# Moving one group's transfers ahead of the weights, and reordering the first two groups of a fused attention and state-space kernel

## The chip, the cores and the metric

The kernel runs on one core of a Trainium2 chip. The time is the device time of one execution in microseconds (us). The engines of the core are PE (TensorE, matrix multiply, with its weight loads shown apart as PEld), DVE (VectorE), ACT (ScalarE), POOL (GpSimd) and SP (SyncE, which here only issues transfers). Each engine works through its own instructions in order. Transfers (DMAs) are issued by SP, ACT or GpSimd and carried out by 16 DMA engines that all of them share.

## What is computed

A gated linear attention over 4 batches, 8 heads, 768 positions and a head size of 48, and then a gated state-space layer on its output:

```python
for t in range(S):                        # attention, per batch and head
    state = alpha[t][:, None] * state + outer(k[t], v[t])
    y[t] = q[t] @ state
x = y.transpose(0, 2, 1, 3).reshape(B, S, H * D)      # (4, 768, 384)
proj = x @ w_in                           # 384 x 1024
val, gate = proj[..., :512], proj[..., 512:]
a = exp(A_log)[0]                         # one decay for all channels
h[t] = a * h[t - 1] + val[t]
out = (silu(gate) * h) @ w_out            # 512 x 384
```

The weights `w_in`, `w_out` and `A_log` arrive as 8-byte words and are turned into float32 on the core.

## The kernel before

**Groups.** The 4 x 768 positions are cut into 12 groups of 256, numbered 0 to 11 (m for the attention of a group, n for its state-space part), each of two chunks (c = 0, 1) of 128 positions. Three groups make one batch.

**Attention of a group.** Alpha, k and q are brought into a layout with head channels on the partitions. For groups 0 to 2 this is done by PE transposes (`natural_alpha`, L572, and `natural_qk`, L589, results called `tn`); from group 3 on DVE transposes (`products`, L616, line L620). `products` then makes running products of alpha (`prod`, the scan of L629) and their inverses (`inv`, the scan of L641), and Z holds k times `inv` and q times `prod` (L603 for groups up to 2, L652 later). Per chunk there follow:

- `keys` (L659): PE turns the k half of Z (`tp`), ACT copies it to `ktm`;
- `scores` (L668): PE multiplies the k half with the q half of Z (`sc`, two PSUM banks);
- `masks` (L678): the causal mask, `A` from `sc`. For group 1 and chunk 1 of group 0 DVE multiplies both banks by the mask (L683). Otherwise ACT copies one bank (L685), GpSimd multiplies that one (L686), and DVE does the other (L687);
- `values` (L689), `state` (L713) and `carried` (L701): PE products that give y and the running state `st`.

**From y to x.** `join` (L724) copies y of a group out of PSUM (`y_sb`, ACT) and writes it in the order of the channels of x as `xT`. Heads 0 and 4 are copied by ACT (L737); the other six need eight moves, since two of them cross a boundary of 128 partitions. These eight are DMAs (L743). Group 0 and group 2 issue them from GpSimd, all others from SP.

**State-space part.** `block(n, cc)` for cc = 0 to 3: `project` (L751) multiplies xT by w_in (`pv`, `pg`), `hidden` (L765) is DVE's scan over time (`hh`, L767), and `gate` (L772) makes f = silu(pg) x hh: ACT and then GpSimd (L778, L779), but for group 0 ACT in place and then DVE (L915, L775). `output` (L786) multiplies f by w_out, copies and stores.

**Weights.** `load_w_in(i)` (L440) issues two DMAs of 384 KB, i = 0 to 3; `load_w_out` (L446) two of 768 KB in all. A weight unit (four of w_in, two of w_out) is rebuilt by `low_word` (ACT, L512), `high_word` (DVE, L526 and L528: two operations, or four through a PSUM bank when `banks` is given) and `word_sum` (GpSimd, L535, one instruction for each half).

**Order.** The order on every engine is written out by hand (a manual schedule): the engines work in the order of the program's text. From the start it is: loads of alpha, k, q, v of groups 0 and 1 and all of w_in on SP (L814 to L824; one chunk of alpha and A_log on ACT); alpha, k, q of group 0; then w_out and alpha of group 2 on SP; attention of group 0 and its `join`; transposes of k and q of group 1, two filler matmuls (`warm`), Z of group 1, words of unit 0, scores, masks and keys of group 1, words of units 1 and 2, `join` of group 1, then SP's loads of k, q and v of group 2; four blocks of group 0 with words of units 3 to 5 between them; alpha of group 2; loads of group 3; `output(0)`. After that a loop runs over n = 1 to 11, in which the attention of group n + 1, the products of group n + 2 and the blocks of group n are interleaved. SP's loads and moves are in one queue, in the order of the text. PSUM tiles with the tag `mm` (pv, pg, o, tp) share three buffers.

Of the kernel before, what the change touches and what calls it, by code (L numbers as in the profile page):

```python
# [13 lines left out]
AF = mybir.ActivationFunctionType  # L14
# [332 lines left out]
def fast(  # L347
# [18 lines left out]
    nc = tc.nc  # L366
    B, H, S, D = q.shape
    DM = H * D
    DI = moe_A_log.shape[0]
    C = 128  # L370
    G = 2
# [68 lines left out]
    def load_w_in(i, engine):  # L440
        for vg in range(2):
            engine.dma_start(out=bits_in[i][:, :, vg].rearrange("p kk n two -> p kk (n two)"),
                             in_=moe_w_in.bitcast(U32)[:, ds(2 * (vg * DI + i * C), 2 * C)]
                             .rearrange("(kk p) n -> p kk n", p=C))

    def load_w_out(i, engine):  # L446
        engine.dma_start(out=bits_out[:, ds(2 * i, 2)].rearrange("p cc n two -> p cc (n two)"),
                         in_=moe_w_out.bitcast(U32)[ds(2 * C * i, 2 * C)].rearrange("(cc p) n -> p cc n", p=C))
# [59 lines left out]
    def low_word(i):  # L508
        lo, _, w = unit(i)
        _, x, y, z = w.shape  # L510
        wrs[i] = p4.tile([C, x, y, z], I32, tag="wr", name="wr")
        nc.scalar.activation(wrs[i], lo, AF.Copy, scale=2.0 ** -29)  # L512

    def high_word(i, banks=None):

        _, hi, w = unit(i)
        t = w.bitcast(U32)
        if banks is None:
            parts = [(hi, t, t)]
        elif i < NI:  # L520
            parts = [(hi[:, :, vg], banks[vg][:, 0:NK], t[:, :, vg]) for vg in range(2)]
        else:
            parts = [(hi[:, r, 0], banks[r].rearrange("p h n -> p (h n)")[:, 0:DM], t[:, r, 0])
                     for r in range(2)]
        for h, x, y in parts:
            nc.vector.tensor_scalar(out=x, in0=h, scalar1=3, scalar2=0x3FFFFFFF,  # L526
                                    op0=ALU.logical_shift_left, op1=ALU.bitwise_and)
            nc.vector.scalar_tensor_tensor(out=y, in0=h, scalar=0xC0000000, in1=x,  # L528
                                           op0=ALU.bitwise_and, op1=ALU.bitwise_or)

    def word_sum(i):
        w, r = unit(i)[2].bitcast(I32), wrs.pop(i)
        for half in range(2):
            x, y = (t[:, :, half] if i < NI else t[:, half] for t in (w, r))
            nc.gpsimd.tensor_tensor(out=x, in0=x, in1=y, op=ALU.add)  # L535
# [132 lines left out]
    def scores(m, c):  # L668
        Z = Zs[m]
        cols = ds(c * C, C)  # L670
        sc = [ps_sc.tile([C, 4, C], FP32, tag=f"sc{i}", name=f"sc{i}") for i in range(2)]
        for p in range(4):
            for i in range(2):
                rows = ds(64 * i, D)
                nc.tensor.matmul(sc[i][:, p, :], Z[rows, p, 1, cols], Z[rows, p, 0, cols], start=True, stop=True)  # L675
        As[m, c] = p2.tile([C, 2, 4, C], FP32, tag="A", name="A"), sc

    def masks(m, c):  # L678
        A, sc = As[m, c]
        mb = mask[:, None, :].to_broadcast([C, 4, C])  # L680
        if m == 1 or (m, c) == (0, 1):
            for i in range(2):
                nc.vector.tensor_mul(A[:, i], sc[i], mb)  # L683
            return
        nc.scalar.activation(A[:, 1], sc[1], AF.Copy)  # L685
        nc.gpsimd.tensor_mul(A[:, 1], A[:, 1], mb)  # L686
        nc.vector.tensor_mul(A[:, 0], sc[0], mb)  # L687
# [33 lines left out]
        S_sbs[ch] = p2.tile([C, 4, D], FP32, tag="S_sb", name="S_sb")  # L721
        nc.scalar.activation(S_sbs[ch], st, AF.Copy)

    def join(m, engine):  # L724

        y = ys.pop(m)
        y_sb = p2.tile([C, 4, GC], FP32, tag="y_sb", name="y_sb")
        nc.scalar.activation(y_sb[:, 1::2], y[1], AF.Copy)
        nc.scalar.activation(y_sb[:, 2], y[0][:, 1], AF.Copy)
        xT = xTs[m] = p2.tile([C, NK, GC], FP32, tag="xT", name="xT")  # L730

        def transfers():
            for h in range(H):
                s, a = divmod(h, 4)
                if not a:
                    kk, row = divmod(h * D, C)
                    nc.scalar.activation(xT[ds(row, D), kk], y[0][ds(64 * s, D), 0], AF.Copy)  # L737
                    continue
                d = 0
                while d < D:  # L740
                    kk, row = divmod(h * D + d, C)
                    size = min(D - d, C - row)
                    engine.dma_start(out=xT[ds(row, size), kk], in_=y_sb[ds(64 * s + d, size), a])  # L743
                    d += size
        return transfers


    prev_h = [None] * NI
# [22 lines left out]

    def gate(n, cc, pg):  # L772
        hh = hhs.pop((n, cc))
        if n == 0:
            nc.vector.tensor_mul(fs[n][:, cc, :], hh, pg)  # L775
            return
        sg = p2.tile([C, GC], FP32, tag="sg", name="sg")
        nc.scalar.activation(sg, pg, AF.Silu)  # L778
        nc.gpsimd.tensor_mul(fs[n][:, cc, :], sg, hh)  # L779
# [29 lines left out]
    def pair(name, m, one, other):  # L809
        load_natural(name, m, 0, one)  # L810
        load_natural(name, m, 1, other)
# [8 lines left out]
    pair("k", 1, SP, SP)  # L820
    pair("q", 1, SP, SP)
    load_v(1, SP)
    for i in range(NI):
        load_w_in(i, SP)  # L824

    constants()
    def warm(count):

        t = ps_mm.tile([C, 4, C], FP32, tag="mm", name="warm")
        for _ in range(count):  # L830
            nc.tensor.matmul(t, ident, ident[:, None, :].to_broadcast([C, 4, C]), start=True, stop=True)
# [9 lines left out]
    nc.scalar.activation(a_dec, al, AF.Exp)  # L841
    check_alpha(0)
    k_times, q_times = natural_qk(0, "k"), natural_qk(0, "q")
    for i in range(2):
        load_w_out(i, SP)
    pair("a", 2, SP, SP)

    warm(2)
    evict = natural_alpha(1)
    warm(2)  # L850
# [19 lines left out]
    values(0, 1)  # L870
    state(0, 1)
    carried(0, 1)
    join(0, nc.gpsimd)()
    k_times, q_times = natural_qk(1, "k"), natural_qk(1, "q", ps_mm)
    warm(2)
    for _ in steps:
        pass
    for times in (k_times, q_times):
        for c in range(G):
            times(c)  # L880
    low_word(0)
    high_word(0)
    word_sum(0)


    for c in range(G):
        scores(1, c)
    for c in range(G):
        masks(1, c)
    for c in range(G):  # L890
        keys(1, c)
    low_word(1)
    state(1, 0)
    values(1, 0)
    banks = [ps_sc.tile([C, 4, C], U32, tag=f"sc{i}", name=f"bank{i}") for i in range(2)]
# [1 line left out]
    def words(i):  # L897
        high_word(i, banks)
        word_sum(i)

    words(1)
    values(1, 1)
    state(1, 1)
# [1 line left out]
    words(2)  # L905
    carried(1, 0)
    carried(1, 1)
    join(1, SP)()
    for name in "kq":
        pair(name, 2, SP, SP)  # L910
    load_v(2, SP)
    for cc in range(NI):
        pv, pg = project(0, cc)
        hidden(0, cc, pv)
        nc.scalar.activation(pg, pg, AF.Silu)  # L915
        if cc < NI - 1:
            low_word(cc + 3)
            words(cc + 3)
        gate(0, cc, pg)
# [9 lines left out]
    for n in range(1, N):  # L929
        m = n + 1  # L930
        att = m < N
        steps = products(n + 2) if n + 2 < N else iter(())

        def go(count):
            for _ in range(count):
                next(steps, None)

        def attend():
            if att:
                state(m, 0)  # L940
                values(m, 0)
                values(m, 1)
                state(m, 1)
                carried(m, 0)
                carried(m, 1)
                join(m, nc.gpsimd if m == 2 else SP)()

        if n == 1:
            block(n, 0)
            k_times, q_times = natural_qk(m, "k"), natural_qk(m, "q")  # L950
            for c in range(G):
                k_times(c)
                q_times(c)
            block(n, 1)

        if n + 3 < N:
            loads(n + 3)
        if n + 2 < N:
            load_v(n + 2, SP)
        if att:  # L960
            for c in range(G):
                keys(m, c)
            for c in range(G):
                scores(m, c)
        go(1)
        if att:
            for c in range(G):
                masks(m, c)
        if n > 1:
            block(n, 0)  # L970
            if n == N - 1:
                next(end, None)
            go(1)
            block(n, 1)
            go(1)
            attend()
            go(2)
            block(n, 2)
        else:
            block(n, 2)  # L980
            go(1)
            attend()
            go(1)
        go(1)
        block(n, 3)
        go(10)
        if 3 <= n:
            for _ in itertools.islice(checks, 2):
                pass
        if n == N - 2:  # L990
            end = check_end()
            next(end)
        if n == N - 1:
            value = nc.values_load(flag[0:1, 0:1], min_val=0, max_val=1)
        output(n)
# [39 lines left out]
```

## Time and profile before

| | us (or as noted) |
|---|---|
| median of 3 runs | 297.95 (297.06 to 298.05) |
| profiled execution, device time | 297.63 |
| its span in the profile | 295.9 |
| PE busy | 286.1 (97%) |
| DVE busy | 227.8 (77%) |
| POOL busy | 108.1 (37%) |
| ACT busy | 98.7 (33%) |
| moved by the queue q1 (SP's), of all DMA bytes | 40.81 MB of 42.08 MB |

A row of the timeline reads: start, length, engine, line of the program, operation, what is written and from what, shape, how many instructions are merged, and in brackets how long the engine was idle before and who ended the wait. An engine name with a q stands for its instruction sequencer, as with SPq, which issues DMAs: there the length is the time that issuing took, not the transfer. "To landing" is the time from issue until all parts of a transfer have arrived.

### The profile page before, as it was taken

How to read it: one execution, taken by the hardware profiler on the slowest of the kernel's cores; microseconds unless marked ns; L12 is line 12 of the kernel's file. 1: busy time of each engine (PE TensorE's matmuls, PEld its weight loads, DVE VectorE, ACT ScalarE, POOL GpSimd, SP SyncE). 2: the span in 40 equal slices, each digit the busy share in tenths (PEclk: the TensorE clock that was granted, in tenths of full speed). 3: DMA queues.
4: the chain of work that ended last, by engine and by line, in shares of the span. 5: the costliest groups of instructions: out<-in, count | busy, mean ns of one | idle time of the engine just before them, and what ended most of it. 6: DMA issues, size and time to landing. Idle time of an engine off the chain costs nothing. (4 is left out here: it accounts for less than half of the span.)

```text
span 295.9 us, 6116 instructions
## 1 busy us (share of the span) xinstructions
PE 286.1 (97%) x2347; PEld 226.7 (77%) x2347; DVE 227.8 (77%) x266; ACT 98.7 (33%) x219; POOL 108.1 (37%) x112
## 2 busy tenths in 40 slices
PE   8899999999999999999999999999999999999991
PEld 4577976986886886886886886886886887886870
DVE  4999897799998599699699699699699695312211
ACT  3354644232531531531531531531531531431110
POOL 7028570166423423453423423452423423401110
PEclk9999999999999999999999999999999999999998
DMA  9999959999991891891891693791694401101101
GB/s 129 163 170 304 350 89 160 231 279 228 242 201 39 218 201 38 206 211 39 213 207 36 172 221 64 201 210 44 166 223 67 109 10 35 53 13 29 53 4 62
DMA packets 71150, 42.08 MB, mean 142 GB/s; under 512 B 47492, under 2 KB 70408, under 8 KB 71112
## 3 DMA queue, kind: packets, MB, share of 16 engines
q1 hardware_dynamic: 69552, 40.81, 67.6%
q0 software_dynamic: 512, 0.59, 0.9%
q8 instruction: 20, 0.33, 0.5%
q10 hardware_dynamic: 1048, 0.20, 0.5%
q14 instruction: 18, 0.15, 0.2%
HBM read 33.33 MB, written 4.72 MB: 129 GB/s over the span
## 5 line engine op out<-in xcount | busy, mean ns | idle before, releaser
L779 POOL TENSOR_TENSOR f<-sg,hh 128x256 f32<-128x256 f32 x44 | 56.1, 1275 | 100.0 <-ACT sg L778 50.7
L759 PE MATMUL pv<-xT,w_in 128*128 128x256 f32 x288 | 72.4, 387 | 0.0
L759 PE MATMUL pg<-xT,w_in 128*128 128x256 f32 x288 | 70.3, 380 | 0.0
L792 PE MATMUL o<-w_out,f 128*128 128x384 f32 x192 | 64.0, 486 | 0.0
L759 PEld LDWEIGHTS pg<-xT,w_in 128*128 128x128 f32 x288 | 54.5, 190 | 8.1 <-DVE hh L767 0.8
L759 PEld LDWEIGHTS pv<-xT,w_in 128*128 128x128 f32 x288 | 52.7, 190 | 10.2 <-issue 2.0
L792 PEld LDWEIGHTS o<-w_out,f 128*128 128x128 f32 x192 | 36.4, 190 | 23.0 <-DVE hh L767 0.2
L686 POOL TENSOR_TENSOR A<-A,mask 128x512 f32<-128x512 f32 x21 | 26.8, 1295 | 66.0 <-ACT A L685 66.0
L778 ACT ACTIVATE sg<-pg 128x256 f32<-128x256 f32 x44 | 16.9, 383 | 89.2 <-PE pg L759 89.2
L767 DVE TENSOR_TENSOR_SCAN hh<-a_dec,hh,pv 128x256 f32<-128x256 f32 x32 | 23.3, 727 | 24.3 <-PE pv L759 24.2
L629 DVE TENSOR_TENSOR_SCAN prod<-aT,first 128x1024 f32<-128x1024 f32 x12 | 33.0, 2753 | 0.1
L641 DVE TENSOR_TENSOR_SCAN inv<-aT,last 128x1025 f32<-128x1025 f32 x12 | 30.6, 2547 | 0.4
L687 DVE TENSOR_TENSOR A<-sc,mask 128x512 f32<-128x512 f32 x21 | 14.3, 689 | 18.5 <-PE sc L675 18.4
L797 ACT ACTIVATE o_sb<-o 128x384 f32<-128x384 f32 x22 | 10.8, 490 | 45.2 <-PE o L792 45.2
L675 PEld LDWEIGHTS sc<-Z 48*128 48x128 f32 x384 | 22.4, 188 | 3.2 <-issue 1.7
L675 PE MATMUL sc<-Z 48*128 48x128 f32 x384 | 24.7, 278 | 0.0
L698 PE MATMUL y<-A,v 128*64 128x128 f32 x384 | 23.5, 274 | 0.6 <-DVE A L687 0.6
L698 PEld LDWEIGHTS y<-A,v 128*64 128x64 f32 x384 | 20.7, 137 | 1.0 <-DVE A L687 0.9
L620 DVE STREAM_TRANSPOSE aT<-raw_a 128x1024 f32<-128x1024 f32 x9 | 18.4, 2040 | 0.7 <-DMA raw_a<-in_alpha_dram 0.7
L620 DVE STREAM_TRANSPOSE Z<-raw_q 128x1024 f32<-128x1024 f32 x9 | 18.2, 2020 | 0.0
L620 DVE STREAM_TRANSPOSE Z<-raw_k 128x1024 f32<-128x1024 f32 x9 | 18.2, 2017 | 0.0
L719 PEld LDWEIGHTS st<-v,ktm 128*64 128x64 f32 x320 | 11.4, 137 | 3.9 <-issue 3.3
(95 smaller groups left out, 273.7 us busy)
## 6 DMA issues: line engine op xcount, KB each, us to landing
raw_k<-in_k_dram SPq DMA_DIRECT2D x24, 192.0 KB, 5.2
raw_q<-in_q_dram SPq DMA_DIRECT2D x24, 192.0 KB, 6.1
v<-in_v_dram SPq DMA_DIRECT2D x24, 192.0 KB, 6.9
out_dram<-o_sb SPq DMA_DIRECT2D x24, 192.0 KB, 1.9
raw_a<-in_alpha_dram SPq DMA_DIRECT2D x23, 192.0 KB, 4.4
raw_a<-in_alpha_dram SPq DMA_DIRECT2D x18, 176.0 KB, 4.7
raw_k<-in_k_dram SPq DMA_DIRECT2D x18, 176.0 KB, 5.5
raw_q<-in_q_dram SPq DMA_DIRECT2D x18, 176.0 KB, 6.7
```

What stands on the lines that cost most here:

```text
L620: nc.vector.transpose(out=to.rearrange("p h (c j) -> p h j c", j=NT), in_=raw_bufs[m % NR][name].rearrange("p h (j d) -> p h j d", d=D)[:, ...
L629: nc.vector.tensor_tensor_scan(out=prod, data0=aT[:, 0:4 * GC], data1=first.rearrange("p h n -> p (h n)"), initial=0.0, op0=ALU.mult, op1= ...
L641: nc.vector.tensor_tensor_scan(out=inv[:, ::-1], data0=aT[:, ::-1], data1=last.rearrange("p h n -> p (h n)")[:, 0:4 * GC + 1][:, ::-1], in ...
L675: nc.tensor.matmul(sc[i][:, p, :], Z[rows, p, 1, cols], Z[rows, p, 0, cols], start=True, stop=True)
L686: nc.gpsimd.tensor_mul(A[:, 1], A[:, 1], mb)
L687: nc.vector.tensor_mul(A[:, 0], sc[0], mb)
L698: nc.tensor.matmul(ys[m][i][ds(64 * s, 64), e, ds(c * C, C)], v_sb[:, c, 2 * p + i, :], A[:, i, p, :], start=(c == 0 and e == 0), stop=Fal ...
L759: nc.tensor.matmul(pj, w_in[cc][:, kk, vg, :], xT[:, kk, :], start=(kk == 0), stop=(kk == NK - 1))
L767: nc.vector.tensor_tensor_scan(out=hh, data0=a_dec[:, cc:cc + 1].to_broadcast([C, GC]), data1=pv, initial=prev_h[cc][:, GC - 1:GC] if n % ...
L778: nc.scalar.activation(sg, pg, AF.Silu)
L779: nc.gpsimd.tensor_mul(fs[n][:, cc, :], sg, hh)
L792: nc.tensor.matmul(os[c], fs[n][:, cc, ds(c * C, C)], w_out[:, cc, :], start=(cc == 0), stop=(cc == NI - 1))
```

## The change

- `masks`: group 1 no longer has both banks on DVE; only chunk 1 of group 0 has. Group 1 takes the way through ACT and GpSimd.
- `join`: takes two issuing engines, one for heads 1 to 3 and one for heads 5 to 7, issues at once, ACT's two copies first, and goes over the heads in the order 1, 5, 3, 7, 2, 6. Group 0 uses SP and GpSimd (four DMAs each), group 2 GpSimd for all, every other group SP for all.
- Loads: before the start of the computation SP issues only unit 0 of w_in. Units 1 to 3 of w_in, w_out and alpha of group 2 are issued after the `join` of group 0.
- Group 1: no filler matmuls; Z, keys, scores and masks are issued chunk by chunk; unit 0 of the weights is rebuilt after the masks instead of before the scores, and through PSUM banks.
- `gate`: group 0 is made like all others, with ACT's silu into `sg` and the product on GpSimd.

```diff
     def masks(m, c):
...
-        if m == 1 or (m, c) == (0, 1):
+        if (m, c) == (0, 1):
...
-    def join(m, engine):
+    def join(m, engines):
...
         xT = xTs[m] = p2.tile([C, NK, GC], FP32, tag="xT", name="xT")
-
-        def transfers():
-            for h in range(H):
-                s, a = divmod(h, 4)
-                if not a:
-                    kk, row = divmod(h * D, C)
-                    nc.scalar.activation(xT[ds(row, D), kk], y[0][ds(64 * s, D), 0], AF.Copy)
-                    continue
-                d = 0
-                while d < D:
-                    kk, row = divmod(h * D + d, C)
-                    size = min(D - d, C - row)
-                    engine.dma_start(out=xT[ds(row, size), kk], in_=y_sb[ds(64 * s + d, size), a])
-                    d += size
-        return transfers
+        for h in (0, 4):
+            kk, row = divmod(h * D, C)
+            nc.scalar.activation(xT[ds(row, D), kk], y[0][ds(16 * h, D), 0], AF.Copy)
+        for h in (1, 5, 3, 7, 2, 6):
+            s, a = divmod(h, 4)
+            d = 0
+            while d < D:
+                kk, row = divmod(h * D + d, C)
+                size = min(D - d, C - row)
+                engines[s].dma_start(out=xT[ds(row, size), kk], in_=y_sb[ds(64 * s + d, size), a])
+                d += size
...
     def gate(n, cc, pg):
         hh = hhs.pop((n, cc))
-        if n == 0:
-            nc.vector.tensor_mul(fs[n][:, cc, :], hh, pg)
-            return
...
     load_v(1, SP)
-    for i in range(NI):
-        load_w_in(i, SP)
+    load_w_in(0, SP)
...
     k_times, q_times = natural_qk(0, "k"), natural_qk(0, "q")
-    for i in range(2):
-        load_w_out(i, SP)
-    pair("a", 2, SP, SP)
-
...
     carried(0, 1)
-    join(0, nc.gpsimd)()
+    join(0, (SP, nc.gpsimd))
+    for i in range(1, NI):
+        load_w_in(i, SP)
+    for i in range(2):
+        load_w_out(i, SP)
+    pair("a", 2, SP, SP)
     k_times, q_times = natural_qk(1, "k"), natural_qk(1, "q", ps_mm)
-    warm(2)
     for _ in steps:
         pass
-    for times in (k_times, q_times):
-        for c in range(G):
-            times(c)
-    low_word(0)
-    high_word(0)
-    word_sum(0)
-
 
     for c in range(G):
-        scores(1, c)
-    for c in range(G):
-        masks(1, c)
+        k_times(c)
+        q_times(c)
     for c in range(G):
         keys(1, c)
-    low_word(1)
+        scores(1, c)
+        masks(1, c)
+    low_word(0)
     state(1, 0)
     values(1, 0)
...
+    words(0)
+    low_word(1)
     words(1)
...
-    join(1, SP)()
+    join(1, (SP, SP))
...
         hidden(0, cc, pv)
-        nc.scalar.activation(pg, pg, AF.Silu)
...
-                join(m, nc.gpsimd if m == 2 else SP)()
+                join(m, (nc.gpsimd, nc.gpsimd) if m == 2 else (SP, SP))
```

## The prediction

> **What bounds the kernel now.** First the page's slices and then stretches: busy time of every engine in the four stretches that matter. Columns are the stretch, then the busy microseconds of PE, PEld, DVE, ACT, POOL, the granted clock, the DMA share and GB/s.
>
> ```profile
> 45.00:57.70 12.70, 12.70 (x62) 9.72 (x60) 9.14 (x12) 3.29 (x8) 0.73 (x1) 1.00 1.19 200
> 57.70:74.70 17.00, 17.00 (x162) 13.26 (x160) 16.72 (x16) 6.62 (x16) 10.46 (x13) 1.00 1.12 250
> 74.70:97.00 22.30, 22.30 (x186) 17.87 (x184) 20.19 (x20) 7.86 (x19) 7.73 (x6) 1.00 0.74 153
> 97.00:119.00 22.00, 22.00 (x197) 17.86 (x196) 19.57 (x18) 7.20 (x18) 7.72 (x6) 1.00 0.74 153
> ```
>
> From 45 us on, PE is busy in every microsecond. In the steady groups (from 74.7) DVE has about 2 us of slack in 22, so PE sets the pace and whatever PE loses or gains before 74.7 stays in the total. But between 57.7 and 74.7 DVE is full as well (16.72 of 17.00), so I read that stretch next, DVE first and then the weight loads of PE (start, duration, instruction, idle time before it and who ended it).
>
> ```profile
> 56.25 0.74 DVE L767 TENSOR_TENSOR_SCAN hh<-a_dec,hh,pv 128x256 f32<-128x256 f32 x1
> 57.73 2.07 DVE L620 STREAM_TRANSPOSE aT<-raw_a 128x1024 f32<-128x1024 f32 x1 [0.74 <-DMA raw_a<-in_alpha_dram]
> ...
> 62.05 2.86 DVE L629 TENSOR_TENSOR_SCAN prod<-aT,first 128x1024 f32<-128x1024 f32 x1
> 64.95 0.51 DVE L638 TENSOR_SCALAR ratio<-prod 128x4 f32<-128x4 f32 x1
> ...
> 69.65 0.67 DVE L767 TENSOR_TENSOR_SCAN hh<-a_dec,hh,pv 128x256 f32<-128x256 f32 x1
> ...
> 73.41 1.23 DVE L652 TENSOR_TENSOR Z<-Z,prod 128x1024 f32<-128x1024 f32 x1
> ```
>
> ```profile
> 70.37 2.99 PEld L792 LDWEIGHTS o<-w_out,f 128*128 128x128 f32 x10 [0.23 <-DVE hh L767]
> ...
> 74.78 1.31 PEld L675 LDWEIGHTS sc<-Z 48*128 48x128 f32 x22 [0.17 <-issue]
> ```
>
> DVE waited 0.74 us for alpha of group 3 (landed about 57.65) and then ran without a hole to the end of Z of group 3, 73.41 + 1.23 = 74.64. PE needs that chain twice: its output matmuls at 70.37 waited for the hh that ended at 70.32, and the scores of group 3 start at 74.78, 0.14 us after Z. Both meetings are tight to 0.2 us. So the landing of alpha(3) is a bound of its own, as tight as PE. What is behind it is SP's queue (issue times; SP issues every large load, in order).
>
> ```profile
> 17.99 6.94 SPq L442 DMA_DIRECT2D bits_in<-in_moe_w_in_dram x8
> 24.98 2.35 SPq L447 DMA_DIRECT2D bits_out<-in_moe_w_out_dram x2
> 27.45 7.44 SPq L421 DMA_DIRECT2D raw_a<-in_alpha_dram x2
> 34.98 8.08 SPq L743 DMA_DIRECT2D xT<-y_sb x8
> 43.16 1.82 SPq L421 DMA_DIRECT2D raw_k<-in_k_dram x2
> 45.07 1.55 SPq L421 DMA_DIRECT2D raw_q<-in_q_dram x2
> 46.72 2.90 SPq L430 DMA_DIRECT2D v<-in_v_dram x2
> 49.71 2.52 SPq L406 DMA_DIRECT2D raw_a<-in_alpha_dram x4
> ```
>
> SP is held at alpha(2) for 7.44 us. I read this as a full queue: DMA share is 1.00 in 25 to 30 and 1.08 in 30 to 35, and alpha(2) lands 11.7 to 12.1 us after its issue, at 39.5 and 40.2. Then the eight moves of y of group 1 go out, k of group 2 follows at 43.16, and from 45 to 57.7 the DMA share is 1.19. The train w_in, w_out, alpha(2), y(1), k, q, v of group 2, alpha(3) is one serial thing, and its end is where DVE waits.
>
> In the early part PE (gaps and fillers) is the other thing to see.
>
> ```profile
> 24.01 1.88 PE L831 MATMUL warm<-ident 128*128 128x512 f32 x4
> 25.82 2.06 PE L675 MATMUL sc<-Z 48*128 48x128 f32 x32
> ...
> 33.04 1.56 PE L759 MATMUL pv<-xT,w_in 128*128 128x256 f32 x6
> ```
>
> The last move of y(0) is issued by GpSimd at 26.94 and lands 6.2 us later, at 33.1: the first projection, at 33.04, meets it exactly.
>
> **What the Trainium skill says.** "DMA: Bandwidth & Descriptors", section "Issuing engines are not separate DMA queues": transfers of all issuing engines run on the same 16 DMA engines and interleave, so more queues save only issuing time. The trace agrees so far: y(0) from GpSimd lay in flight among w_in and took a median 6.1 us, y(1) and later from SP 2.0. Same page, "Latency and other measured facts": a fixed cost of about 2 us for a DMA, a first byte after about 1 us from GpSimd. In the trace GpSimd's first move takes 7.0 us in a full queue; what it takes in an empty one no row shows. "SBUF — State Buffer", section "SBUF: two separate sides": GpSimd and a DVE instruction with two SBUF inputs exclude each other for the whole instruction. The trace agrees: beside DVE's prod scan the f of GpSimd takes 2.23 us instead of 0.73, and the scan 2.86 instead of 2.29. "TensorE: Matmul & The Clock Gate", Part 1: idle PE can lose its clock. PEclk is 9 in all slices but the last (8), and 1.00 in the stretches; two filler matmuls less should not change that.
>
> **The change part by part.**
>
> 1. *PE 24 to 33.* The two fillers (24.01 to 25.82) go. Keys of chunk 0 need only k of chunk 0: tn of q ends near 24.0, keys 0.55 (half of 1.09), scores 1.0, keys, scores: 27.1 instead of 28.9. What is late next: the state matmuls need the ktm copy (done), values need the masks. DVE does two masks in place of four (minus 2 x 0.60), ACT two copies of 0.58 more, GpSimd two masks of about 1.27 more, after its four issues of 0.5 that end near 25.3. GpSimd: copy of chunk 0 at 26.3, masks 27.7 and 29.3. PE: state 27.1, values to about 29.9, state 0.55, carried 1.0: first projection at about 31.4, 1.6 us earlier. Its y(0) is there (issued by 25.5).
>
> 2. *High words of block 0* are now four operations of 0.53 us pace in place of 0.58 + 0.96 us, +0.57 us on DVE, against minus 1.2 of masks. w_in 0 landed at 25.1.
>
> 3. *f of block 0 on GpSimd:* DVE loses 4 x 0.33 us of pace; GpSimd gains 4 x 0.73. DVE pays 2.72 us per block in place of 3.05 and is the bound of 33 to 44 (words 4 x 0.53, hh 0.61). GpSimd: 12 half sums of 1.0 and four f from 29.3, 44.2 at the earliest. PE reaches the output of group 0 near 44.0 to 45.6, against 45.11: from 1.1 us early to 0.5 us late, the latter if w_in comes late (step 4).
>
> 4. *SP's order.* SP goes w_in 0 (issued by 20.93), then waits for y_sb of group 0 (22.34 + 0.60 = 22.94), issues four moves at the pace that y(1) shows (3.1 us for the last five, 0.63) to about 25.5, and only now w_in 1 to 3, w_out, alpha(2): six of w_in's eight DMAs, 2.3 MB, start 4.5 us later than the 20.98 of before. First bytes come about 1.5 us after issue (estimate: k of group 2, issued at 43.16, lands 4.0 us later, and 192 KB take 1.2 us at 160 GB/s), so 27.0. Before, the first half of w_in 1 landed at 20.98 + 5.2 = 26.2 and took 1.35 us (384 KB at about 290 GB/s), so the DMA engines began it near 24.9. Hole: 2.1 us. The SP half of y(0), 192 KB, fills 0.66 us of it: 1.45 us of DMA time is lost in a stretch in which before there was none. Bounds: 0.8 if GpSimd's half also falls into the hole, 2.1 if first bytes take as long as 1.8 us and y(0) lies beside the end of w_in 0. Total bytes are the same. So alpha(2) lands 1.45 us later, y(1) (ready by 35) goes out later behind it, k(2) at 44.6, and alpha(3) lands at 59.1. I assume it passes on one to one, because the train from 45 on is full.
>
> 5. *DVE 57.7 to 74.7* starts 1.45 us later. Of this the scan (2.86 against 2.29) and the ratio (0.51 against 0.17) can give back up to 0.9 us if GpSimd's f no longer falls beside them; f waits for hh, which moves with DVE, so I take 0.3. PE stands at the output of group 1 and at the scores of group 3 for 1.15 us plus all that it gained before: gains of steps 1 to 3 buy nothing here.
>
> 6. *Later groups:* the moves of y keep count and size, in another order, with two copies of ACT in the same place; next projections come some 10 us later. Nothing.
>
> Sum: profiled execution 297.63 us (span 295.9 and 1.7 around it) + 1.15 = 298.8. The median of the runs shown is 297.95, 0.3 above the profiled one, so 299.1.
>
> **Rivals.** *Slower by the train (forecast):* chance 0.55, from 298.85 to 300.4 by the bounds of step 4 (0.8 to 2.1) plus up to 0.4 if w_in late also pushes block 0.
>
> *No change, 0.27, 297.1 to 298.8:* the hole is mostly filled, or only one lagging DMA engine made alpha(3) late before (its four parts land at 5.2 to 5.8 us, and a wait is for the last engine), or DVE gets its 0.9 us back. For it: all of this lies within 1.5 us. Against: the share of 1.00 leaves no reserve.
>
> *Faster, 0.18, about 296.9 (to 296.2):* SP is not held by a full queue but by PE. The waits of SP's queue name it:
>
> ```profile
> SPq L421 <- PE pv L759: 6.2, 1, 6.2
> ```
>
> If alpha(2) really went out when the first pv ended (34.6), then SP's train starts with the first projection, which comes 1.6 us earlier; alpha(3) would land up to 1.6 earlier, DVE could take 0.74 of it before it runs into its own hh, and PE with its own gain of about 1.1 would be 0.7 to 1.1 earlier: 297.95 minus 1.0. It decides once alpha(3) lands before 57.0. Against it: alpha(2) overwrites a buffer that PE read at 5 to 7 us, and the next instruction, the first move of y(1), is held too (5.4 us to landing against 2.0).
>
> *That the change does not do what it says:* y(0) over GpSimd may still take 6 us after issue, 25.3 + 6 = 31.3, and so be no earlier than the first projection wants it. That costs PE up to 0.5 us in step 1 and nothing in the end, as long as alpha(3) decides.
>
> **How the numbers follow.** Faster by over 0.3% (0.9 us, about what a measurement of this kernel can tell from none): 0.18; within: 0.27; slower: 0.55. The predicted time is 299.1. The range reaches from 297.0, which holds the no-change case and leaves most of the faster one out, to 300.4. The likeliest case's own range is 298.85 to 300.4.
>
> **What would show it.** Right: w_in 1 issued after 25, a dip of the DMA share at 25 to 27, k(2) after 44, DVE's transpose of alpha(3) after 58.4 with a wait over 1.5 us, PE waiting over 1 us for DVE between 69 and 76, and the first projection before 32.5. Wrong: alpha(3) landing at 57.7 or before, or PE without a wait there; then PE's gain of step 1 comes through and the time falls to 297 or less. Also wrong would be a projection later than 33, which would say that step 1 is mis-sized.

## The result, and the profile after

| | before | after |
|---|---|---|
| median, us (22 runs each) | 297.86 | 297.75 |
| lowest and highest | 296.85, 299.32 | 296.98, 300.05 |
| span of the profiled execution | 295.9 | 296.0 |

The ratio is 1.0001, 95% interval 0.9986 to 1.0017: no change, where 299.1 and "slower" were forecast. Below, a ratio is also given in us, as its distance from 1 times 297.9.

SP's issues in the changed kernel, from the timeline of its queue:

```profile
17.99 2.79 SPq L442 DMA_DIRECT2D bits_in<-in_moe_w_in_dram  x2
22.30 2.51 SPq L740 DMA_DIRECT2D xT<-y_sb  x4
24.85 3.26 SPq L442 DMA_DIRECT2D bits_in<-in_moe_w_in_dram  x6
...
35.45 9.04 SPq L740 DMA_DIRECT2D xT<-y_sb  x8
44.59 1.16 SPq L421 DMA_DIRECT2D raw_k<-in_k_dram  x2
...
49.95 2.47 SPq L406 DMA_DIRECT2D raw_a<-in_alpha_dram  x4
```

w_in 1 goes out at 24.85 (forecast: about 25.5), alpha(2) has landed at about 41.7 instead of 40.2 (forecast: 1.45 later), and k(2) is issued at 44.59, 1.43 later than before (forecast: 1.45). But the last line is the surprise: alpha(3) is issued at 49.95, only 0.24 after the 49.71 of before.

The stretches of the changed kernel (columns as in the prediction):

```profile
24.00:33.00 9.00, 8.83 (x142) 7.70 (x143) 6.28 (x12) 4.53 (x8) 5.87 (x7) 1.00 0.83 248
33.00:45.00 12.00, 10.12 (x49) 7.98 (x48) 11.00 (x21) 7.06 (x13) 11.06 (x13) 1.00 0.77 219
45.00:57.70 12.70, 12.70 (x64) 9.70 (x65) 9.41 (x12) 3.40 (x8) 1.92 (x4) 1.00 1.19 187
57.70:74.70 17.00, 16.79 (x160) 12.89 (x158) 16.74 (x15) 6.21 (x15) 11.35 (x13) 1.00 1.10 243
```

and the first two of these of the kernel before:

```profile
24.00:33.00 9.00, 8.69 (x142) 6.90 (x140) 8.62 (x16) 3.25 (x6) 7.40 (x11) 1.00 1.01 309
33.00:45.00 12.00, 11.88 (x61) 9.79 (x56) 10.77 (x22) 6.77 (x14) 7.85 (x8) 1.00 0.67 183
```

The DMA share of 24 to 33 falls from 1.01 to 0.83. That is the forecast hole: 0.18 of 9 us is 1.6 us. What was not forecast is the second row: PE is busy for 10.12 of 12.00 us instead of 11.88. The weight loads of PE say where:

```profile
30.86 1.16 PEld L755 LDWEIGHTS pv<-xT,w_in 128*128 128x128 f32 x6 [0.18 <-POOL w_in L535]
...
36.28 1.16 PEld L755 LDWEIGHTS pg<-xT,w_in 128*128 128x128 f32 x6 [1.61 <-POOL w_in L535]
...
44.33 0.42 PEld L578 LDWEIGHTS tn<-ident,raw_a 128*128 128x128 f32 x4 [0.88 <-DVE hh L763]
44.71 4.82 PEld L785 LDWEIGHTS o<-w_out,f 128*128 128x128 f32 x16
...
72.54 0.94 PEld L785 LDWEIGHTS o<-w_out,f 128*128 128x128 f32 x4 [0.83 <-POOL f L772]
...
75.20 1.89 PEld L675 LDWEIGHTS sc<-Z 48*128 48x128 f32 x32 [0.47 <-PE tp L665]
```

The first projection starts 2.18 us earlier than the 33.04 of before. Some 0.7 of that is not the change's: ACT's copy of y of group 0 began at 22.34 in the profiled execution of the kernel before and at 21.67 in that of the changed one. The difference is there by the first scan of DVE (8.09 and 7.08), long before the first changed line is reached, and in the profiles of all versions shown here this copy begins anywhere from 21.67 to 22.34. From the copy to the first projection it is 10.70 us before and 9.19 after, so 1.51 us are the change's.

By the output of group 0 the lead is 0.37 (44.71 against 45.08). PE stood at 36.28 and at 44.33, and both times for DVE's `hh`. For 36.28 the row of the weight loads names a word sum of GpSimd, but the sums of unit 1 had ended at 34.47; the row of the matmul itself names the wait:

```profile
36.31 1.53 PE L755 MATMUL pg<-xT,w_in 128*128 128x256 f32 x6 [1.24 <-DVE hh L763]
```

`pv` and `pg` share three PSUM buffers, so `pg` of block 1 takes the buffer of `pv` of block 0, and that one is free when DVE's first `hh` has read it, at 36.17.

From the output of group 0 to the scores of group 3 it is 29.70 us in the kernel before (45.08 to 74.78) and 30.49 in the changed one (44.71 to 75.20). Wherever PE waits nowhere in between for over 0.25 us, the distance is 29.70 or 29.71 in every profile here, so the changed kernel lost 0.79 us there in its profiled execution. What DVE and ACT waited for in the changed kernel:

```profile
31.17 0.56 DVE L526 TENSOR_SCALAR bank<-bits_in 128x384 uint32<-128x384 uint32 x1 [1.43 <-DMA bits_in<-in_moe_w_in_dram]
...
35.49 0.68 DVE L763 TENSOR_TENSOR_SCAN hh<-a_dec,pv 128x256 f32<-128x256 f32 x1
...
57.75 2.07 DVE L620 STREAM_TRANSPOSE aT<-raw_a 128x1024 f32<-128x1024 f32 x1 [1.12 <-DMA raw_a<-in_alpha_dram]
59.85 1.27 DVE L626 TENSOR_TENSOR first<-aT,start_p 128x4 f32<-128x4 f32 x1
...
73.86 1.23 DVE L652 TENSOR_TENSOR Z<-Z,prod 128x1024 f32<-128x1024 f32 x1
```

```profile
31.16 0.92 ACT L512 ACTIVATE wr<-bits_in 128x768 int32<-128x768 uint32 x1 [2.74 <-DMA bits_in<-in_moe_w_in_dram]
33.34 0.93 ACT L512 ACTIVATE wr<-bits_in 128x768 int32<-128x768 uint32 x1 [1.04 <-DMA bits_in<-in_moe_w_in_dram]
```

DVE and ACT (in its first line) stood for w_in 1; ACT's second line is the low word of unit 2. On DVE the words of units 1 and 2 stand ahead of the first `hh`, which therefore comes at 35.49. And alpha(3) is transposed at 57.75, against 57.73 before: of a delay of 1.43 us at k(2), 0.02 is left between these two profiles. DVE's longer wait (1.12 instead of 0.74) only says that DVE came 0.36 earlier.

### The profile page after: what moved, and what is told of

It reads as the page before. It is cut to its first block, busy times and chain, and to the rows that moved or that the text cites. A ratio compares the mean times of both kernels' runs of the same rounds, so it can differ in the third digit from the quotient of the medians.

```text
span 296.0 us, 6116 instructions
## 1 busy us (share of the span) xinstructions
PE 284.0 (96%) x2343; PEld 224.8 (76%) x2343; DVE 226.2 (76%) x262; ACT 100.4 (34%) x221; POOL 113.4 (38%) x114
## 5 line engine op out<-in xcount | busy, mean ns | idle before, releaser
L772 POOL TENSOR_TENSOR f<-sg,hh 128x256 f32<-128x256 f32 x48 | 61.3, 1277 | 97.1 <-ACT sg L771 54.8
L686 POOL TENSOR_TENSOR A<-A,mask 128x512 f32<-128x512 f32 x23 | 28.8, 1271 | 67.5 <-ACT A L685 67.5
L771 ACT ACTIVATE sg<-pg 128x256 f32<-128x256 f32 x48 | 18.4, 384 | 91.5 <-PE pg L755 89.3
L629 DVE TENSOR_TENSOR_SCAN prod<-aT,first 128x1024 f32<-128x1024 f32 x12 | 32.1, 2676 | 0.1
L687 DVE TENSOR_TENSOR A<-sc,mask 128x512 f32<-128x512 f32 x23 | 15.7, 690 | 20.1 <-PE sc L675 20.0
```

Of the source, the lines that this page charges most:

```text
L629: nc.vector.tensor_tensor_scan(out=prod, data0=aT[:, 0:4 * GC], data1=first.rearrange("p h n -> p (h n)"), initial=0.0, op0=ALU.mult, op1= ...
```

## The experiments

Two readings stood against each other (where the first expectations use letters, A is the first and B the second): alpha(3) decides the time, as steps 4 and 5 of the prediction have it; or the late w_in takes in block 0 what steps 1 and 3 gain, and alpha(3) plays a small part.

**Alpha(3) earlier, and w_in 1 earlier.** Alpha(3) is loaded behind q(2) and ahead of v(2):

```diff
     for name in "kq":
         pair(name, 2, SP, SP)
+    load_raw("a", 3, [SP])
     load_v(2, SP)
...
-    loads(3)
+    for name in "kq":
+        load_raw(name, 3, [SP])
```

and w_in 1 ahead of the moves of y(0), in the changed kernel:

```diff
     load_w_in(0, SP)
+    load_w_in(1, SP)
...
     join(0, (SP, nc.gpsimd))
-    for i in range(1, NI):
+    for i in range(2, NI):
         load_w_in(i, SP)
```

Alpha(3) earlier in the changed kernel:

> The changed kernel with alpha of group 3 issued ahead of v of group 2, nothing else. Theory A (the landing of alpha(3) is what cuts off the gain of the change): DVE's transpose of alpha(3) starts at 56.7 instead of 57.75, its wait of 1.12 us goes, PE's waits near 72.5 and 75.2 (0.83 and 0.3 us) go, and the time falls by 1.0 to 1.3 us, to about 296.6. Theory B (what PE gains early is already lost by 45 us, to the late w_in 1): alpha(3) comes earlier, DVE waits less, but PE has nothing to give, within 0.3 us of 297.75.

Alpha(3) earlier in the kernel before:

> The kernel before with alpha of group 3 issued ahead of v of group 2, nothing else. Theory A: PE waited only 0.23 us for DVE here, so even with DVE free 0.74 us earlier the time falls by no more than 0.2 to 0.4 us, to about 297.5; the changed kernel with the same edit is then 0.7 to 1.0 us faster than this one. Theory B: both edited kernels equal, about 297.6.

w_in 1 earlier in the changed kernel:

> The changed kernel with units 0 and 1 of w_in ahead of the moves of y(0), so that the DMA engines have work while SP waits for y. Theory A: no hole in the DMA share at 25 to 27, DVE's wait of 1.43 us for w_in 1 and PE's of 1.24 and 0.64 us go, k(2) is issued about 1 us earlier than 44.6, alpha(3) lands 0 to 0.7 us earlier; time down 0 to 0.7 us, since alpha(3) still decides. Theory B: PE's gain at 45 us (about 1.4 us) passes on whole, time down 1.2 to 1.5 us, to 296.4.

Both in the changed kernel:

> Both edits at once. Theory A: the two work on the two sides of one meeting and add up to more than each: PE early and alpha(3) early, 1.5 to 2.3 us down, to about 295.8. Theory B: no more than with units 0 and 1 ahead alone.

| | median, us | ratio to before (interval) |
|---|---|---|
| after, alpha(3) earlier | 297.82 | 0.9992 (0.9979 to 1.0006) |
| before, alpha(3) earlier | 298.11 | 1.0003 (0.9987 to 1.0019) |
| after, w_in 1 earlier | 296.70 | 0.9960 (0.9943 to 0.9977) |
| after, both | 296.13 | 0.9940 (0.9921 to 0.9960) |

Alpha(3) alone earns nothing that these intervals show, in either kernel, although in both traces DVE no longer waits for it. In the trace of the changed kernel the lost 0.79 us do come back:

```profile
74.47 1.86 PEld L675 LDWEIGHTS sc<-Z 48*128 48x128 f32 x32 [0.17 <-issue]
```

These are the scores of group 3, at 75.20 without the move. The medians (297.82 and 297.75) do not follow. From the two ratios and their intervals the gain is estimated at 0.3 us, give or take 0.6, so a part of it may be real.

One unit of w_in earns 1.2 us (0.7 to 1.7). With it DVE's first `hh` comes 1.49 us earlier than in the changed kernel; the other lines are PE's weight loads:

```profile
34.00 0.68 DVE L763 TENSOR_TENSOR_SCAN hh<-a_dec,pv 128x256 f32<-128x256 f32 x1
...
43.23 4.82 PEld L785 LDWEIGHTS o<-w_out,f 128*128 128x128 f32 x16
...
69.35 2.88 PEld L785 LDWEIGHTS o<-w_out,f 128*128 128x128 f32 x10 [1.06 <-DVE hh L763]
```

The output of group 0 comes at 43.23, 1.48 earlier than in the changed kernel, and now PE has a lead that alpha(3) can take: 1.06 us go at 69.35, behind DVE, which had waited 1.18 for alpha(3). The edit also issues k(2) earlier, at 43.20 instead of 44.59; but alpha(3) earlier by itself gave no such gain. With both moved DVE's wait is gone from the trace, and the time is the lowest measured. So alpha(3) does bound PE in this trace. That moving it earns time here is not shown: the intervals of 296.70 and 296.13 overlap.

**The change in parts.** "Transfers" is the new `join` and the order of SP's loads alone; "order" is group 1 chunk by chunk with its masks, fillers and words; "f" is this:

```diff
     def gate(n, cc, pg):
         hh = hhs.pop((n, cc))
-        if n == 0:
-            nc.vector.tensor_mul(fs[n][:, cc, :], hh, pg)
-            return
...
         hidden(0, cc, pv)
-        nc.scalar.activation(pg, pg, AF.Silu)
```

Each part was put on the kernel before. The transfers there, with the new `join`:

```diff
-    for i in range(NI):
-        load_w_in(i, SP)
+    load_w_in(0, SP)
...
-    for i in range(2):
-        load_w_out(i, SP)
-    pair("a", 2, SP, SP)
...
-    join(0, nc.gpsimd)()
+    join(0, (SP, nc.gpsimd))
+    for i in range(1, NI):
+        load_w_in(i, SP)
+    for i in range(2):
+        load_w_out(i, SP)
+    pair("a", 2, SP, SP)
```

and the order, with the masks:

```diff
-        if m == 1 or (m, c) == (0, 1):
+        if (m, c) == (0, 1):
...
     for c in range(G):
-        scores(1, c)
-    for c in range(G):
-        masks(1, c)
+        k_times(c)
+        q_times(c)
     for c in range(G):
         keys(1, c)
-    low_word(1)
+        scores(1, c)
+        masks(1, c)
+    low_word(0)
...
+    words(0)
+    low_word(1)
     words(1)
```

> Of the change only the transfers: moves of y(0) over SP and GpSimd, ahead of units 1 to 3 of w_in, w_out and alpha(2); the order of group 1, its masks and f of block 0 stay as before. Theory of the prediction (the SP order is the whole cost, passed on by alpha(3)): k(2) about 1.4 later, alpha(3) transposed at 59.1, +1.15 us. New theory (late w_in costs by way of the words, DVE waiting for w_in 1, and PE then for DVE in group 0; alpha(3) passes on little): first projection 0.5 to 1 earlier than 33.04 at most, as the old order of group 1 is the longer one, DVE waits over 1 us for w_in 1, and the output of group 0 at 45.3 to 46.3 against 45.08; time +0.2 to +1.2 us. No effect: if y(0) early buys as much as w_in late costs, within 0.3 us.

> Of the change only the order of group 1 (Z, keys, scores, masks by chunks, masks shared with ACT and GpSimd, no fillers, words after it); transfers and f of block 0 stay as before. Prediction's step 1: PE is ready for the first projection 1.6 us earlier, but y(0) over GpSimd lands at 33.1, so it stands there and nothing is gained before: first projection 33.0, output of group 0 at 45.1 within 0.4, time within 0.4 us. Rival: the words, now behind the masks on DVE and GpSimd, come later and hold block 0: output of group 0 at 45.6 or later and +0.4 to +1 us. Other rival: y(0) lands earlier too as GpSimd's queue is freer, first projection at 31.5 to 32.5, and up to 1 us gained.

> Of the change only f of block 0 on GpSimd. Prediction's step 3: DVE saves 4 x 0.33 us in 33 to 44, where it is the bound; output of group 0 up to 1.1 us early or 0.5 us late, as GpSimd's f stands behind half sums of words. If DVE is the bound of block 0: output at 44.0 to 44.5 instead of 45.08, then alpha(3), as before at 57.7, takes up to 0.3 of the gain: time -0.4 to -1.1 us. If PE or the words on GpSimd are the bound: output at 45.0 to 45.6 and no change within 0.4 us.

And order and f together, which is the change without its transfers:

> The change without its transfers: order of group 1 and f of block 0 as in the change, moves of y(0) on GpSimd and all of w_in ahead as before. Asks whether y(0) ahead of w_in earns anything. If the late w_in is only a cost (1.2 us, as the run with w_in 1 ahead of y(0) gained): first projection 31.5 with a wait of 0.9 us for y(0), output of group 0 at 43.2 to 44.0, alpha(3) transposed near 56.2, and time -0.8 to -1.5 us against the kernel before. If y(0) ahead is worth about what w_in late costs: no change within 0.4 us, as the whole change.

| part, on the kernel before | median, us | ratio to before (interval) | in us |
|---|---|---|---|
| transfers | 301.73 | 1.0108 (1.0067 to 1.0149) | +3.2 |
| order | 297.96 | 1.0005 (0.9997 to 1.0013) | +0.1 |
| f | 297.80 | 0.9989 (0.9973 to 1.0004) | -0.3 |
| order and f | 296.93 | 0.9960 (0.9950 to 0.9971) | -1.2 |
| all three (the change) | 297.75 | 1.0001 (0.9986 to 1.0017) | 0.0 |

The order by itself earns nothing. In its profile the first projection starts early, at 31.49, but then stands for a move of y(0):

```profile
33.13 0.30 PEld L759 LDWEIGHTS pv<-xT,w_in 128*128 128x128 f32 x2 [0.91 <-DMA xT<-y_sb]
```

The transfers alone are the one thing here that costs much. Their six runs are spread: two are below 299.5 and four above 301.4, and the profiled one (302.04) is of the four. What the engines show there, ACT first and then PE:

```profile
32.59 0.89 ACT L512 ACTIVATE wr<-bits_in 128x768 int32<-128x768 uint32 x1 [2.96 <-DMA bits_in<-in_moe_w_in_dram]
```

```profile
33.76 0.55 PEld L719 LDWEIGHTS st<-v,ktm 128*64 128x64 f32 x16 [2.36 <-ACT S_sb L722]
36.00 2.17 PEld L755 LDWEIGHTS pv<-xT,w_in 128*128 128x128 f32 x6 [0.36 <-issue]
...
49.04 4.81 PEld L788 LDWEIGHTS o<-w_out,f 128*128 128x128 f32 x16 [0.17 <-issue]
```

In the old order the low words of w_in 1 stand on ACT ahead of the copy of group 1's state (`S_sb`). ACT waits 2.96 us for w_in 1, the copy waits behind it, PE's attention of group 1 waits for the copy, and the first projection, whose y had been moved early, starts at 36.00 instead of 33.04. By the output of group 0 the delay is 3.96 us (49.04 against 45.08). The new order puts the words behind the attention. There the late w_in holds only block 0, and costs 1.2 us: the difference between order and f with the transfers (ratio 1.0001) and without (0.9960), and what w_in 1 alone gave back. The two cases are not quite alike: w_in 1 came at 32.6 in the one profile and at 31.2 in the other, and transfers and order without f, which would separate f's part, were not run. Nothing is seen that y(0) ahead of w_in would have earned: with w_in 1 ahead and y(0) over two queues the ratio is 0.9960, and without any of the transfers it is the same. Without the transfers the first projection starts at 31.67, with a hole of 0.32 in it:

```profile
31.67 0.73 PEld L759 LDWEIGHTS pv<-xT,w_in 128*128 128x128 f32 x4 [0.18 <-POOL w_in L535]
32.72 0.30 PEld L759 LDWEIGHTS pv<-xT,w_in 128*128 128x128 f32 x2 [0.32 <-issue]
...
43.37 4.82 PEld L789 LDWEIGHTS o<-w_out,f 128*128 128x128 f32 x16
...
68.60 3.05 PEld L789 LDWEIGHTS o<-w_out,f 128*128 128x128 f32 x10 [0.17 <-DVE hh L767]
```

**Who takes the gain of f.** With f alone PE reaches the output of group 0 at 44.15, 0.93 early. Then, PE first and DVE second:

```profile
70.28 2.88 PEld L789 LDWEIGHTS o<-w_out,f 128*128 128x128 f32 x10 [1.06 <-DVE hh L767]
```

```profile
57.58 2.06 DVE L620 STREAM_TRANSPOSE aT<-raw_a 128x1024 f32<-128x1024 f32 x1 [1.52 <-DMA raw_a<-in_alpha_dram]
```

That looks like alpha(3). To test it, alpha(3) was moved in the kernel with f alone, first ahead of k(2) and then, as above, behind q(2). Ahead of k(2):

```diff
+    load_raw("a", 3, [SP])
     for name in "kq":
         pair(name, 2, SP, SP)
...
-    loads(3)
+    for name in "kq":
+        load_raw(name, 3, [SP])
```

> The kernel before with f of block 0 on GpSimd and alpha(3) loaded ahead of k(2). Alone, f brought PE 0.93 us ahead at the output of group 0 and PE lost 1.06 at 70.28 waiting for hh, behind DVE, which had waited 1.52 for alpha(3). If alpha(3) is the bound that takes the gain of f: no wait of DVE for alpha(3), no wait of PE over 0.4 at the output of group 1, time -0.7 to -1.1 us. Rival: something else of DVE (its 16.7 of 17.0 busy us from 57.7 on) is the bound: PE waits as long, and the time stays within 0.4 us of before.

> The kernel before with f of block 0 on GpSimd and alpha(3) loaded behind q(2) and ahead of v(2). If alpha(3) takes f's gain: DVE waits under 0.5 us for it, PE waits under 0.4 at the output of group 1, PE's lead of 0.9 at the output of group 0 stays to the scores of group 3 (73.9 instead of 74.78), time -0.5 to -1.0 us. If DVE itself is the bound there: scores at 74.5 or later and within 0.4 us.

Ahead of k(2) it earned nothing: 298.24, ratio 0.9999 (0.9982 to 1.0016). It had pushed q(2) back, and PE stood there instead:

```profile
53.11 0.42 PEld L597 LDWEIGHTS tn<-ident,raw_q 128*128 128x128 f32 x4 [0.68 <-DMA raw_q<-in_q_dram]
...
54.31 0.42 PEld L597 LDWEIGHTS tn<-ident,raw_q 128*128 128x128 f32 x4 [0.79 <-DMA raw_q<-in_q_dram]
```

Behind q(2), 296.82, ratio 0.9968 (0.9958 to 0.9977): -1.0 us, where f alone gave -0.3 and alpha(3) alone +0.1, both within their intervals of nothing. DVE and PE have no such waits left:

```profile
55.51 2.06 DVE L620 STREAM_TRANSPOSE aT<-raw_a 128x1024 f32<-128x1024 f32 x1
```

```profile
68.86 3.06 PEld L789 LDWEIGHTS o<-w_out,f 128*128 128x128 f32 x10 [0.17 <-DVE hh L767]
```

So in the kernel before PE's lead and alpha(3) are two bounds at the same place; lifting one shows the other.

**How much delay the train takes.** Small loads into a tile that nobody reads hold SP ahead of k(2), in the kernel before:

```diff
     join(1, SP)()
+    idle = const.tile([NI, C], FP32, name="idle")
+    for _ in range(3):
+        SP.dma_start(out=idle, in_=moe_A_log.rearrange("(a p) -> a p", p=C))
     for name in "kq":
         pair(name, 2, SP, SP)
```

Three, then one and six:

> The kernel before with three small loads of A_log (2 KB each, into a tile that nobody reads) on SP ahead of k(2), so that SP's loads of group 2 and alpha(3) are issued later and nothing else is changed: each takes SP some 0.6 us, so k(2) is issued 1.5 to 1.9 later than 43.16. Prediction's step 4 (one to one): alpha(3) is transposed at 59.2 to 59.6, +1.2 to +1.6 us. Elastic train: the transfers of 45 to 57.7 run below their limit or SP's issues catch up, so alpha(3) is transposed before 58.5 and the time rises by under 0.6 us.

> The kernel before with one small load instead of three on SP ahead of k(2): k(2) 0.6 to 1.3 us later than 43.16. Reserve of about 1.4 us: alpha(3) transposed at 57.4 to 57.9 (57.73 before), time within 0.3 us. Constant fraction of 0.4: 58.0 to 58.3 and +0.3 to +0.6 us. One to one: 58.3 to 59.0, and +0.6 to +1.3 us.

> The same with six small loads: with one held issue of 1.2 us and the others at 0.3 to 1.3 us, k(2) 4 to 6.5 us later. Reserve of about 1.4 to 1.6 us, then in full: alpha(3) 2.5 to 5 us later and the time up by about as much. Constant fraction of 0.4: alpha(3) 1.6 to 2.6 later and the time up by that.

| | k(2) issued | alpha(3) transposed | between | median, us | ratio (interval) |
|---|---|---|---|---|---|
| before | 43.16 | 57.73 | 14.57 | | |
| the change | 44.59 | 57.75 | 13.16 | 297.75 | 1.0001 (0.9986 to 1.0017) |
| one load | 43.31 | 56.79, no wait | | 297.75 | 0.9996 (0.9982 to 1.0009) |
| three | 45.83 | 58.79 | 12.96 | 299.22 | 1.0052 (1.0033 to 1.0071) |
| six | 51.03 | 63.71 | 12.68 | 303.66 | 1.0202 (1.0174 to 1.0229) |

The line of DVE with six loads:

```profile
63.71 2.05 DVE L620 STREAM_TRANSPOSE aT<-raw_a 128x1024 f32<-128x1024 f32 x1 [3.16 <-DMA raw_a<-in_alpha_dram]
```

One load moved k(2) by only 0.15, too little for a test of delay. But its profile is a second look at nearly the same train, and there alpha(3) was issued at 48.84 (49.71 before) and transposed at 56.79, without a wait. Its four parts took 5.4 to 5.7 us to land there and 5.2 to 5.8 before; what differs is how soon SP issued them. So alpha(3) came about 1 us earlier in an execution that loads nearly the same, and the time did not move with it.

A reserve here is a delay of k(2) that does not reach alpha(3). Its size depends on the profile that one counts from. From that of before, a delay of 2.67 at k(2) becomes 1.06 at alpha(3) and a delay of 7.87 becomes 5.98: a reserve of 1.6 to 1.9 us. From that with one load, 2.52 becomes at least 2.00 and 7.72 at least 6.92: a reserve of at most 0.5 to 0.8. Between three and six loads 4.92 of 5.20 pass on, whichever is taken. A constant fraction of 0.4 would have made 2.1 of the 5.20.

The times do not hang on one profile. They rise by 1.55 us (1.0 to 2.1) with three loads and by 6.0 (5.2 to 6.8) with six, which is 1.1 and 1.9 less than the delay of k(2) in the profiles. By the first of these the change's 1.43 would cost some 0.3 us (estimate: 1.43 less 1.1). With six loads it is not alpha(3) alone: PE waited 0.8 to 1.1 us for each half of k(2) and q(2), and was 3.6 us late already at the scores of group 2.

**Towards a better version.** Order and f with alpha(3) ahead of k(2), and behind q(2), by the edits above; and the changed kernel with alpha(3) behind q(2) and two units of w_in ahead of y(0):

```diff
     load_w_in(0, SP)
+    load_w_in(1, SP)
+    load_w_in(2, SP)
```

> As the change without its transfers, with alpha(3) ahead of k(2). If PE's lead of block 0 is now held to the end: 1.4 to 1.9 us faster than before, as the run with w_in 1 and alpha(3) both early (-1.76). If y(0) ahead of the rest of w_in is worth something by itself: 0.5 us or more slower than that run.

> The change without its transfers, with alpha(3) behind q(2) and ahead of v(2). Without the move alpha(3) came at 55.79 and DVE waited only 0.51 for it, and PE nowhere over 0.2 between the output of group 0 and the scores of group 3. So nothing is left to gain: 296.4 to 297.1, as without it (296.93). Rival: DVE's half us helps, 296.0 to 296.4, as the run with w_in 1 and alpha(3) early.

> The changed kernel with units 1 and 2 of w_in ahead of the moves of y(0) and alpha(3) ahead of k(2). If unit 2 of w_in late is also waited for: up to 0.4 us faster than the run with unit 1 ahead (296.1), 295.7 to 296.1. If SP's moves of y(0) then come too late behind it in the DMA engines: first projection at 32 or later, and 296.3 to 297.0.

The expectation of the last says "ahead of k(2)"; its edit puts alpha(3) behind q(2). They gave 298.13 (1.0004, 0.9990 to 1.0018), 296.36 (0.9955, 0.9944 to 0.9967) and 296.67 (0.9956, 0.9942 to 0.9971). The first lost its 1.2 us to q(2) again (PE waits of 0.52 and 0.79). The other two and the version with w_in 1 and alpha(3) earlier (296.13) cannot be told apart by their intervals. All three beat the kernel before, by 1.3 to 1.8 us, and so the changed one, which is as fast as it. Alpha(3) behind q(2) added nothing measurable to order and f (0.9955 against 0.9960), as expected, and a second unit of w_in ahead of y(0) brought nothing more.

## Why the prediction was wrong

The step that failed is step 4's last: "I assume it passes on one to one, because the train from 45 on is full". It made 1.45 us at alpha(3) out of 1.45 at k(2), and step 5 made 1.15 us of time out of that. The runs showed k(2) 1.43 us late, as forecast, and alpha(3) 0.02 later than in the profile of before; taking alpha(3) out of the way (behind q(2), 297.82) gave the changed kernel no measurable gain, 0.9 us at the very most; and a delay of 2.67 us at k(2), forced on the kernel before, cost 1.55. That the time did not change is the sum of two other things: order and f earn 1.2 us, and the late w_in 1 takes 1.2 us back in block 0.

- *Step 1 (first projection 1.6 us earlier, at 31.4)* was right: 1.51 by the distance from y's copy; the 30.86 has the earlier start of that execution in it. That y(0) over GpSimd might still take 6 us did not come true. Its two 48-KB moves took a median 1.9 us to landing.
- *Step 2 (+0.57 and -1.2 us on DVE)* was not taken apart by a run of its own.
- *Step 3 (output of group 0 at 44.0 to 45.6, DVE the bound of the stretch)* was right: 44.71, inside the range because w_in 1 was late, and PE stood for DVE. Without the transfers it is 43.37. The step reserved up to 1.6 us for a late w_in, and that case came true with 1.34 (44.71 less 43.37). But it was carried into the sum as worth nothing, or at most 0.4 us.
- *Step 4* was right in the hole and at alpha(2) and k(2). One term is off: SP's half of y(0) is 144 KB (two moves of 48, one of 32, one of 16), not 192, so it fills 0.5 us of the hole and 1.6 are left, which is what the DMA share shows. The 1.43 at k(2) are also not the hole alone: SP was free of alpha(2) only 0.47 us later (35.36 against 34.89), and the moves of y(1) took it 0.96 longer (9.04 against 8.08). That the two together make the forecast 1.45 is in part luck. What failed is the sentence above: a share of 1.19 between 45 and 57.7 was read as no reserve.
- *Step 5* did not come into play as a cost of 1.15 us, but its mechanism holds: where alpha(3) was transposed later, with three and six loads, the scores of group 3 moved with it (76.02 and 80.85 against 74.78), and the time rose. In the profile of the change 0.79 us go to this chain, which the medians neither confirm nor exclude.
- *"Gains of steps 1 to 3 buy nothing here"* is half right. They buy 1.2 us with the transfers left out. In the change they are spent by the late w_in in block 0, not at alpha(3). The forecast followed the moved loads to the last transfer of the train, and only named what they do to their first consumers, the words of w_in 1 on ACT and DVE.
- *The rivals.* "No change" came true. Of its three reasons none is shown as it stood: the hole was not filled. DVE's later scan fell to 2.27 us while its `first` grew by 1.10. And a lagging DMA engine is not what made alpha(3) late before: its parts landed as fast as in the profile with one load, but were issued 0.87 later. That alpha(3) was late by chance in the profile of before stays possible. The low end of the likeliest range, 298.85, does not come from the bound of 0.8 us, which gives 298.75 at most (297.95 + 0.8). "Faster" named the first projection as what holds SP at alpha(2); against it, SP was held there until 35.36, later than before (34.89), though the projection came 2.18 earlier.

What stays open is how large the reserve is and what it consists of. Part is seen in SP's queue: k, q and v of group 2 took from 43.16 to 49.71 before and from 44.59 to 49.95 after, the same issues in 1.2 us less; with one load it was 5.5 us instead of 6.6. What held SP there was not tried. Open is also how much of the 0.79 us at alpha(3) the typical execution of the change loses; beside the late alpha(3) it holds the wait of `first` described below, and no run took that away by itself.

## What to carry to other kernels

When loads are moved behind something, price first what stands on the queues of their first consumers: these transfers cost 3.2 us where the words of w_in stood ahead of the attention, and 1.2 us where they stood behind it. A wait of 0.7 us for the end of a long train of transfers does not say that the train passes delays on: delay it by a known amount and see. One profile is not enough to count from: in two profiles with nearly the same train DVE began on its last load 0.94 us apart. And when two bounds meet within a microsecond, test them together, since each alone earns nothing.

## What the runs showed of the hardware

DVE's `first`, four columns, took 1.27 us in the changed kernel. In the kernel before, and beside it GpSimd in the changed kernel:

```profile
59.83 0.17 DVE L626 TENSOR_TENSOR first<-aT,start_p 128x4 f32<-128x4 f32 x1
```

```profile
59.84 2.50 POOL L686 TENSOR_TENSOR A<-A,mask 128x512 f32<-128x512 f32 x2 [1.47 <-ACT A L685]
```

GpSimd's first mask began at 59.84, 0.01 us ahead of `first`; in the kernel before it began at 60.27, after `first` had ended. The Trainium skill, "SBUF — State Buffer", section "SBUF: two separate sides", says that of a DVE instruction with two SBUF inputs and a GpSimd one that reads SBUF, whichever starts first has the shared ports for its whole length. The trace agrees, with 1.10 us on an instruction of 0.17: a shift of 0.4 us of GpSimd decided it.

GpSimd's moves of 48 KB took 6.3 us to landing behind all of w_in and 1.9 with only w_in 0 ahead of them. The Trainium skill, "DMA: Bandwidth & Descriptors", section "Latency and other measured facts", gives a fixed cost of about 2 us; the second number agrees.

The small loads held SP for 3.05 us (three) and 7.15 us (six), one alone for 0.54. Most of that is not their issuing, which took 0.25 to 0.54 us each: they write one tile, and each waited for the one before it to land, 1.8 us in two waits and 5.0 in five.
